# Attention with one pool of seven PSUM banks, and four and two row maxima in alternate steps

## The chip, the cores and the metric

The kernel runs on one core of a Trainium2 chip. The metric is the device time of one execution in microseconds; three executions of the kernel before took 3544.29 to 3546.45 us, with a median of 3546.07. The engines are TensorE (PE; its weight loads are shown as PEld), VectorE (DVE), ScalarE (ACT), GpSimd (POOL) and SyncE (SP, which here only issues DMAs). TensorE writes to PSUM, which has eight banks of 512 floats on each of 128 partitions; VectorE and ScalarE read it.

## The reference

Two layers of two sublayers each, on 2048 rows of 512 values in float32:

```python
x = x + fnet(layernorm(x))       # Re(DFT over rows of the DFT over columns)
x = x + attention(layernorm(x))  # 32 query heads of 16, one key head, one value head
# and both once more

q = heads(x @ wq); k = x @ wk; v = x @ wv
p = softmax(q @ k.T / 4)          # for each head, 2048 x 2048
o = concat(p @ v) @ wo
```

The softmax takes the row maximum off before the exponential, so each score is computed twice: once with queries on the partitions, for the maximum of each row, and once with keys on the partitions, for the exponential and the product with v.

## The kernel before, in words

Instructions are issued in the order in which the Python code names them; each engine works through its own in that order, and waits are put in where data or a buffer is not ready. There are two functions for each layer. `phase_a` computes the Fourier sublayer, the layer norms, and q, k and v. `phase_b` is the attention. Where a matmul of `phase_a` leaves room, `pump` and `issue` (lines 445 to 493) already put in some of the row maxima, by an estimate of when banks come free.

`phase_b` (line 1132) walks through 16 query tiles of 128 rows, and through each tile in 32 steps: two halves of the heads, times 16 tiles of 128 keys. One step has, in this order:
- the value product of two steps earlier (`pv`, line 987): four matmuls in four column groups of the array, into the one bank `z`, where they add up over the 16 key tiles;
- four score matmuls (`score`, line 963), each on 64 of the 128 array rows, so that two can run side by side on the two row halves. Two of them fill the two banks of one `pair()`, and one exponential on ScalarE (line 983) reads both;
- row maxima for later query tiles (`more_max`, line 950): one score matmul on one row half into a bank `y`, and one `reduce_max` on VectorE (line 409).

The maxima are kept at a steady rate: `owed` gives three for each step and six ahead. In a step the order is two scores, two maxima, two scores, one maximum. The row half of the first score is chosen such that matmuls go to the two halves by turns.

PSUM is divided by name: three banks `y` in rotation, two pairs `x` of two banks each in rotation, and one bank `z`. A matmul into a bank waits until the last reader of that bank's former content is done; the wait sits on the weight load ahead of the matmul.

Once for each query tile, in step 13, `o_proj` multiplies the former tile's result with the output weights: twelve matmuls into a bank `y`, and an addition on VectorE (line 1056). Where all maxima are done (the end of the last tile), the second pair of scores goes to two banks `y`, with one exponential for each (lines 971 to 976).

At the end of `phase_a`, four row tiles (12 to 15) are handled more finely: `root`, `ln_inv` and `apply` give their layer norm, `tr` transposes them through bank `z`, `q_half` computes queries, and `q_split` splits them into a rounded part and a low part that GpSimd computes (line 376). `keep` takes a bank `y` ahead of time for k, v or q, and `kept` hands it out.

Of the kernel before, what the change touches and what calls it, by code (L numbers as in the profile page):

```python
# [17 lines left out]
P = 128  # L18
# [29 lines left out]
def fnet_mqa_kernel(ctx: ExitStack, tc: tile.TileContext, x_in, ct, dt_, wq, wkv, wo, out):  # L48
# [6 lines left out]
    def f(ap):  # L55
        return ap.bitcast(F32)
# [139 lines left out]
    def make_layer(L, src, mid, dst, last):  # L196
# [76 lines left out]
                split_ps(v[0], xth, xtl)  # L273

        def keep(after):
            st["pk"], st["kept"] = bank("y"), 3
            held("y", clk["pe"] + 1.4 + 2.8 + after)

        def kept():
# [47 lines left out]
        def q_mm(tb, g, xth, xtl):  # L327
            wh, wl = st["wqh", g]
            pq = kept()
            spend(pe=2.9, act=1.2)  # L330
            for k in range(NK):
                ks = slice(k * P, (k + 1) * P)
                mm3(pq, wh[:, ks], wl[:, ks], xth[:, k, :], xtl[:, k, :], k == 0, k == NK - 1)
            hi = half(4 + 2 * (g % 2), F32R)
            lo = half(5 + 2 * (g % 2), F32R)
            split_act(pq, hi, lo, sb.tile([P, D], F32, name="qraw"))
            st["qs", tb, g] = hi, lo

        def q_half(t0, g, xth, xtl, between=lambda: None):
# [26 lines left out]
        def q_split(t0, g, pq):  # L366
            if g == 0:
                st["raw"] = half(6)
                if t0 == 14:
                    st["stage"] = slot(3, F32R)  # L370
            hl = half((4, 5, 0, 1)[g], F32R) if t0 == 12 else st["stage"][:, g * 512:(g + 1) * 512]
            raw = st["raw"][:, 256 * (g % 2):256 * (g % 2) + 256]
            nc.scalar.copy(raw, pq)
            nc.scalar.copy(hl[:, :256], raw)
            st["qs", t0, g] = hl
            sub = lambda: nc.gpsimd.tensor_sub(hl[:, 256:], raw, f(hl[:, :256]))
            (st["subs"].append(sub) if t0 == 14 and g > 1 else sub())

        def q_half_store(t0, g):
            hl = st["qs", t0, g]  # L380
# [22 lines left out]
            return o.mxp[i]  # L403

        def max_of(i, pr, g, c0, n, to, tag="y"):
            pm = bank(tag)[:, :n]
            gs = slice(64 * g, 64 * g + KR)
            nc.tensor.matmul(pm, o.qT[i][gs, pr, :], kz[gs, c0:c0 + n], start=True, stop=True)  # L408
            nc.vector.reduce_max(to, pm, axis=AX.X)  # L409
# [268 lines left out]
        def prep_tasks(tb, x1):  # L678
# [42 lines left out]
            ts[6, 0] = [lambda: (kv_lo(4 * tb, 4), k_diff(tb) if tb < 2 else None), hold]  # L721
# [11 lines left out]
        def phase_a(extra):  # L733
            tasks = {}

            def add(n, fn):
                tasks.setdefault(n, []).append(fn)
# [116 lines left out]
            for n in range(128):  # L854
# [47 lines left out]
                if n % 32 == 31 and tb < 3:  # L902
# [33 lines left out]
            take(mb, 99)  # L936
            max_neg(0, 0, HALF, 5)
            max_rows_pe(0, 0, HALF)
            for sub in st["subs"]:
                sub()  # L940
            for k in range(6):
                more_max()

# [8 lines left out]
                max_half(*units[o.done])  # L952
                o.done += 1

        def owed(n):
            return min(3 * (n + 1) + 6, len(units)) - o.done

        def done_with(i, pr):
            return all(u[:2] > (i, pr) for u in units[o.done:])
# [3 lines left out]
        def score(i, s_, j):  # L963
            hf, c = divmod(s_, NT)
            jj, g = divmod(j, 2)
            cp = 4 * (2 * hf + jj)
            if (i, s_) not in ptiles:
                k = i * NSTEP + s_
                ptiles[i, s_] = slot((6, 7, 2)[k % 3]).rearrange("p (j n) -> p j n", j=4)
            w = j // 2  # L970
            if i == NT - 1 and jj == 1 and o.done == len(units):
                e = bank("y")
                nc.tensor.matmul(e, kz[64 * g:64 * g + KR, c * P:(c + 1) * P],
                                 o.qT[i][64 * g:64 * g + KR, cp:cp + 4, :], start=True, stop=True)
                nc.scalar.activation(ptiles[i, s_][:, j, :], e, AF.Exp, scale=DH ** -0.5)
                return
            first = "e" not in st
            if first:
                st["e"] = pair()
            nc.tensor.matmul(st["e"][:, g, :], kz[64 * g:64 * g + KR, c * P:(c + 1) * P],  # L980
                             o.qT[i][64 * g:64 * g + KR, cp:cp + 4, :], start=True, stop=True)
            if not first:
                nc.scalar.activation(ptiles[i, s_][:, 2 * w:2 * w + 2, :], st.pop("e"), AF.Exp, scale=DH ** -0.5)  # L983

        acc = {}

        def pv(i, s_):
            hf, c = divmod(s_, NT)
            if c == 0:
                acc[i, hf] = bank("z")  # L990
            a = acc[i, hf]
            pt = ptiles.pop((i, s_))
            for j in range(4):
                nc.tensor.matmul(a[32 * j:32 * j + 32, :], v1[:, c, :], pt[:, j, :], start=c == 0, stop=c == NT - 1)  # L994
# [48 lines left out]

        def o_mm(k):
            if k == 0:
                bt["po"] = bank("y")
# [85 lines left out]
        def phase_b(nxt):  # L1132
# [5 lines left out]
                nc.sync.dma_start(st["wo", j], wo[:, j, :])  # L1138

            behind = []  # L1140
            for n in range(NT * NSTEP):
                i, s_ = divmod(n, NSTEP)
                if len(behind) == 2:
# [43 lines left out]
                nxt.a_start()  # L1187
            for at in behind:
                pv(*at)
            return {**out_tasks(NT - 1), 12: [lambda: o_proj(NT - 1)]}  # L1190

        def half_tasks(i):
# [63 lines left out]
```

## Time and profile before

| what | value |
|---|---|
| median of three executions | 3546.07 us |
| profiled execution, its own time | 3549.72 us |
| its span | 3547.9 us |
| TensorE busy | 3505.9 us, 99% |
| VectorE busy | 2714.7 us, 77% |
| ScalarE busy | 2503.3 us, 71% |
| first and last value product of all | 640.7 and 3538.1 us |

Times in the profile's rows are microseconds from the start of the span; the number after a bar and a comma is the mean duration of one instruction in nanoseconds. "idle before <- X" is the time in which the engine stood still just before these instructions, and X is what ended it. A matmul's end is modelled, so that a busy TensorE may still have room; the distance between the starts of equal instructions is the surer measure.

### The profile page before, as it was taken

How to read it: one execution, taken by the hardware profiler on the slowest of the kernel's cores; microseconds unless marked ns; L12 is line 12 of the kernel's file. 1: busy time of each engine (PE TensorE's matmuls, PEld its weight loads, DVE VectorE, ACT ScalarE, POOL GpSimd, SP SyncE). 2: the span in 40 equal slices, each digit the busy share in tenths (PEclk: the TensorE clock that was granted, in tenths of full speed). 3: DMA queues.
4: the chain of work that ended last, by engine and by line, in shares of the span. 5: the costliest groups of instructions: out<-in, count | busy, mean ns of one | idle time of the engine just before them, and what ended most of it. 6: DMA issues, size and time to landing. Idle time of an engine off the chain costs nothing.

```text
span 3547.9 us, 64282 instructions
## 1 busy us (share of the span) xinstructions
PE 3505.9 (99%) x24576; PEld 1874.8 (53%) x24576; DVE 2714.7 (77%) x4892; ACT 2503.3 (71%) x3210; POOL 830.5 (23%) x1262
## 2 busy tenths in 40 slices
PE   8999999999999999999999999999999999999999
PEld 6887878433333333333378878883333333333333
DVE  6267776888888888888432777768888888888883
ACT  4223733888888888888932247438888888888888
POOL 4244342211221122112213443422101110111011
PEclk9999999999999999999999999999999999999999
DMA  6435252311111100111144342523111111011100
GB/s 191 150 144 167 80 165 87 85 56 34 35 35 51 36 23 23 49 34 26 40 137 128 127 150 90 153 66 88 47 37 35 49 34 38 23 35 37 37 23 25
DMA packets 224900, 254.55 MB, mean 72 GB/s; under 512 B 52880, under 2 KB 174800, under 8 KB 217424
## 3 DMA queue, kind: packets, MB, share of 16 engines
q1 hardware_dynamic: 210384, 233.12, 21.6%
q0 software_dynamic: 14208, 17.33, 1.6%
q8 instruction: 193, 3.16, 0.4%
q14 instruction: 115, 0.94, 0.1%
HBM read 187.16 MB, written 65.27 MB: 71 GB/s over the span
## 4 chain that ended last, share of the span: by engine, by line
PE 91%; issue 2%; DVE 2%; ACT 2%; POOL 1%; DMA 1%; SPq 0%; ACTq 0%; POOLq 0%; DVEq 0%
PE z L994 29%; PE x L980 19%; PE y L408 13%; PE x L809 11%; PE y L87 3%; PE y L88 3%; PE y L89 2%; PE y L475 2%; PE x L87 2%; PE x L89 2%; PE x L88 2%; PE x L593 1%; PE z L475 1%; DVE row L191 1%; POOL cl L79 1%
## 5 line engine op out<-in xcount | busy, mean ns | idle before, releaser
L983 ACT ACTIVATE slot<-x 128x1024 f32<-128x1024 f32 x2000 | 1945.9, 1024 | 284.5 <-PE x L980 276.2
L409 DVE TENSOR_REDUCE mxp<-y 128x1 f32<-128x512 f32 x2944 | 1849.6, 684 | 181.5 <-PE y L408 168.7
L994 PE MATMUL z<-slot,v 128*32 128x512 f32 x8192 | 1096.3, 605 | 1.6 <-DVE lnv L1105 0.7
L980 PE MATMUL x<-slot,kz 64*128 64x512 f32 x2976 | 677.3, 450 | 2.2 <-DMA slot<-craw 1.7
L980 PEld LDWEIGHTS x<-slot,kz 64*128 64x128 f32 x2976 | 279.2, 184 | 744.7 <-ACT slot L983 685.8
L408 PE MATMUL y<-kz,slot 64*128 64x512 f32 x2176 | 581.6, 397 | 1.9 <-DVE mxp L409 1.9
L809 PE MATMUL x<-cl,xnh 64*128 64x512 f32 (+1 forms) x1536 | 355.8, 357 | 0.0
L994 PEld LDWEIGHTS z<-slot,v 128*32 128x32 f32 x8192 | 163.4, 108 | 363.7 <-issue 332.8
L809 PE MATMUL x<-ch,xnh 64*128 64x512 f32 (+1 forms) x1536 | 348.1, 361 | 2.3 <-ACT row L796 2.2
L809 PE MATMUL x<-ch,xnl 64*128 64x512 f32 (+1 forms) x1536 | 346.2, 362 | 0.9 <-ACT xnl L580 0.9
L408 PEld LDWEIGHTS y<-kz,slot 64*128 64x128 f32 x2176 | 276.7, 186 | 22.8 <-DVE mxp L409 10.8
L79 POOL TENSOR_TENSOR cl<-craw,ch 128x512 fp32r<-128x512 f32 x176 | 223.9, 1295 | 225.5 <-ACT ch L78 174.3
L78 ACT CAST ch<-craw 128x512 fp32r<-128x512 f32 x256 | 154.6, 622 | 170.9 <-PE x L89 87.1
L475 PE MATMUL y<-kz,slot 64*128 64x512 f32 x690 | 271.7, 405 | 2.1 <-ACT rel L479 1.2
L543 POOL DMA_DIRECT2D slot<-mt x224 | 112.1, 508 | 585.2 <-PE y L408 490.1
L809 PEld LDWEIGHTS x<-ch,xnh 64*128 64x128 f32 x1536 | 213.1, 188 | 23.3 <-issue 5.2
L809 PEld LDWEIGHTS x<-cl,xnh 64*128 64x128 f32 x1536 | 217.7, 188 | 12.6
L489 DVE TENSOR_REDUCE mxe<-y 128x1 f32<-128x512 f32 x316 | 198.8, 679 | 29.3 <-PE y L475 28.7
L809 PEld LDWEIGHTS x<-ch,xnl 64*128 64x128 f32 x1536 | 209.7, 187 | 21.1 <-issue 5.9
L1035 POOL TENSOR_TENSOR row<-row,row 128x256 f32<-128x256 f32 x63 | 46.5, 738 | 700.3 <-DMA row<-rd 654.0
L87 PE MATMUL x<-ch,xnh 128*128 128x512 f32 x384 | 154.3, 402 | 9.1 <-ACT ch L78 8.4
L89 PE MATMUL x<-ch,xnl 128*128 128x512 f32 x384 | 153.4, 399 | 2.6 <-POOL xnl L659 2.6
(198 smaller groups left out, 4143.3 us busy)
## 6 DMA issues: line engine op xcount, KB each, us to landing
craw<-ct_in SPq DMA_DIRECT2D x112, 512.0 KB
slot<-qd SPq DMA_DIRECT2D x44, 1024.0 KB
qd<-row SPq DMA_DIRECT2D x144, 128.0 KB
od<-row SPq DMA_DIRECT2D x252, 64.0 KB
row<-wqd SPq DMA_DIRECT2D x48, 256.0 KB
row<-x_in SPq DMA_DIRECT2D x32, 256.0 KB
mid<-row POOLq DMA_DIRECT2D x32, 256.0 KB, 2.4
craw<-ct_in SPq DMA_DIRECT2D x32, 256.0 KB
```

What stands on the lines that cost most here:

```text
L79: (eng or nc.vector).tensor_sub(lo, raw, f(hi))
L87: nc.tensor.matmul(ps_, ah, bh, start=start, stop=False)
L88: nc.tensor.matmul(ps_, ah, bl, start=False, stop=False)
L89: nc.tensor.matmul(ps_, al, bh, start=False, stop=stop)
L408: nc.tensor.matmul(pm, o.qT[i][gs, pr, :], kz[gs, c0:c0 + n], start=True, stop=True)
L409: nc.vector.reduce_max(to, pm, axis=AX.X)
L475: nc.tensor.matmul(pm, o.qT[i][gs, pr, :], k[gs, c0:c0 + 512], start=True, stop=True)
L489: nc.vector.reduce_max(to, pm, axis=AX.X)
L809: nc.tensor.matmul(z[d], a[gs, s, d * P:(d + 1) * P], b[gs, :], start=first and q < 2 and e == 0, stop=last and q > 1 and e == len(turns) - 1)
L980: nc.tensor.matmul(st["e"][:, g, :], kz[64 * g:64 * g + KR, c * P:(c + 1) * P], o.qT[i][64 * g:64 * g + KR, cp:cp + 4, :], start=True, sto ...
L983: nc.scalar.activation(ptiles[i, s_][:, 2 * w:2 * w + 2, :], st.pop("e"), AF.Exp, scale=DH ** -0.5)
L994: nc.tensor.matmul(a[32 * j:32 * j + 32, :], v1[:, c, :], pt[:, j, :], start=c == 0, stop=c == NT - 1)
```

## The change

- PSUM becomes one tile of eight banks. Bank 7 is `z`. In `phase_a`, `pair()` hands out banks 0 and 1, then 2 and 3, by turns, and `bank("y")` hands out 4, 5 and 6 by turns; a bank that `keep` has taken is now passed over (`own`) until its last reader is issued.
- In `phase_b`, scores, maxima and the output projection share banks 0 to 6. Which ones is decided while the program is built, by an estimate of when TensorE's two halves, VectorE and ScalarE are free (`flow`, `take_bank`, `issue_at`). A maximum takes, of the banks that are free by then, the one that came free last; if none is free, the one that comes free first. A pair takes the two neighbours that come free first.
- A step has four, two or no maxima in place of three (`share`). Credit grows in each step by what is needed to meet the next deadline, by 2 at least; at 4 or more the step takes four, else two. The order of scores (s) and maxima (m) is `smmssmms`, `ssmmss` or `ssss`.
- In the last steps, without maxima, every pair of scores has one exponential.
- At the end of `phase_a`, the maxima keep off bank `z` from the middle of task 122 until the transposes of row tile 13 are issued; `root(15)` is issued ahead of the first `q_half(12)`; and the low parts of the first two query groups of tiles 12 and 13 are computed on VectorE, after the second `q_half`.

```diff
+ORDER = {0: "ssss", 2: "ssmmss", 4: "smmssmms"}
...
+    banks = ps.tile([P, 8, 512], F32, name="banks")
+    turns = {"y": 4, "x": 0, "own": None}
...
     def bank(tag):
-        return ps.tile([P, 512], F32, name=tag, bufs={"y": 3, "z": 1}[tag])
+        if tag == "z":
+            return banks[:, 7, :]
+        while True:
+            b = turns["y"]
+            turns["y"] = 4 + (b - 3) % 3
+            if b != turns["own"]:
+                return banks[:, b, :]
...
+    def take_bank(g):
+        fb = flow["free"]
+        t = max(flow["last"], *(flow["half"] if flow["wide"] or g is None else flow["half"][g:g + 1]))
+        ready = [b for b in range(7) if fb[b] + 0.06 <= t and g is not None]
+        return max(ready, key=lambda b: fb[b]) if ready else min(range(7), key=lambda b: fb[b])
+
+    def issue_at(g, bs):
+        h = flow["half"]
+        t = max(h[g], flow["last"], *(flow["free"][b] + 0.06 for b in bs))
+        if flow["wide"]:
+            t = max(t, *h)
+            h[:] = [max(v, t) + 0.195 for v in h]
+            t = h[g]
+            flow["wide"] = False
+        h[g], flow["last"] = t + 0.231, t
+        return t + 0.431
...
     def pair():
-        return ps.tile([P, 2, 512], F32, name="x", bufs=2)
+        turns["x"] ^= 2
+        return banks[:, turns["x"]:turns["x"] + 2, :]
...
         def max_of(i, pr, g, c0, n, to, tag="y"):
-            pm = bank(tag)[:, :n]
+            if flow:
+                b = take_bank(g)
+                ready = issue_at(g, [b])
+                at = max(flow["dve"], ready)
+                flow["dve"], flow["free"][b] = at + 0.605, at + 0.69
+                pm = banks[:, b, :n]
+            else:
+                pm = bank(tag)[:, :n]
...
-            add(123, lambda: tr(13))
+            add(123, lambda: (tr(13), st.update(hold=False)))
+            inner[122, 1] = [lambda: st.update(hold=True)]
...
             tr(14)
+            root(15, 1)
             q_half(12, 0, *xt[0])
-            root(15, 1)
             ln_inv(*st["root"], nc.vector)
             apply(15)
             q_half(12, 1, *xt[0])
+            lows(2)
...
+        def share(n):
+            need = max((c - o.done) / max(1, at - 1 - n) for c, at in goals if at > n or c > o.done)
+            st["due"] = min(st.get("due", 0.0) + max(2.0, need), 6.0)
+            k = 4 if st["due"] >= 4 else 2
+            st["due"] -= k
+            return k
...
             if first:
-                st["e"] = pair()
+                b = min(range(6), key=lambda b: max(flow["free"][b:b + 2]))
+                bs = [b, b + 1]
+                ready = issue_at(g, bs)
+                st["bs"], st["e"] = bs, banks[:, b:b + 2, :]
...
-                g = units[o.done][2] if o.done < len(units) else 1
-                for j, m in ((g, 0), (1 - g, 2), (2 + g, 0), (3 - g, 2)):
-                    score(i, s_, j)
-                    for _ in range(m):
-                        if owed(n) >= 1:
-                            more_max()
+                js = iter((1, 0, 3, 2))
+                for m in ORDER[share(n) if o.done < len(units) else 0]:
+                    more_max() if m == "m" else score(i, s_, next(js))
```

More of the change, by code (lines that the diff above doesn't have):

```diff
@@ L62, in half, with start_flow, own @@
         return sb.tile([P, D], dtype, name=f"row{k}")
+    banks = ps.tile([P, 8, 512], F32, name="banks")
+    turns = {"y": 4, "x": 0, "own": None}
     def bank(tag):
[L65 removed]
+        if tag == "z":
[5 more added lines that the diff above has]
+                return banks[:, b, :]
+    flow = {}
+    def start_flow():
+        flow.update(free=[0.0] * 7, half=[0.0, 0.0], last=0.0, dve=0.0, act=0.0, wide=False, exps=[])
+    def take_bank(g):
[13 more added lines that the diff above has]
+        return t + 0.431
+    def own(ap=None):
+        turns["own"] = None if ap is None else 4 + (turns["y"] - 5) % 3
+        return ap
     def pair():
[L68 removed]
+        turns["x"] ^= 2
+        return banks[:, turns["x"]:turns["x"] + 2, :]
     def split_ps(ps_, hi, lo, neg=False):
@@ L275, in keep @@
         def keep(after):
-            st["pk"], st["kept"] = bank("y"), 3
+            st["pk"], st["kept"] = own(bank("y")), 3
             held("y", clk["pe"] + 1.4 + 2.8 + after)
@@ L953, in more_max @@
                 o.done += 1
-        def owed(n):
-            return min(3 * (n + 1) + 6, len(units)) - o.done
+        goals = []
+        for j in range(NT):
+            for lim in (HALF, NPAIR):
+                at = NSTEP * (j - 1) + NSTEP - AHEAD if j < NT - 2 or lim == HALF else NSTEP * j + NT - AHEAD
+                if j == 0:
+                    at = NT - AHEAD
+                goals.append((sum(u[0] < j or (u[0] == j and u[1] < lim) for u in units), at))
+        def share(n):
[4 more added lines that the diff above has]
+            return k
         def done_with(i, pr):
@@ L970, in score @@
             w = j // 2
[L971 to L976, printed above, removed]
             first = "e" not in st
             if first:
-                st["e"] = pair()
+                b = min(range(6), key=lambda b: max(flow["free"][b:b + 2]))
+                bs = [b, b + 1]
+                ready = issue_at(g, bs)
+                st["bs"], st["e"] = bs, banks[:, b:b + 2, :]
+            else:
+                ready = issue_at(g, [])
+            for b in st["bs"]:
+                flow["free"][b] = 1e9
             nc.tensor.matmul(st["e"][:, g, :], kz[64 * g:64 * g + KR, c * P:(c + 1) * P],
@@ L982, in score @@
             if not first:
+                at = max(flow["act"], ready + 0.03)
+                flow["act"] = at + 0.925
+                for b in st["bs"]:
+                    flow["free"][b] = at + 1.02
+                flow["exps"].append(at + 1.02)
                 nc.scalar.activation(ptiles[i, s_][:, 2 * w:2 * w + 2, :], st.pop("e"), AF.Exp, scale=DH ** -0.5)
@@ L992, in pv @@
             pt = ptiles.pop((i, s_))
+            t = max(flow["half"]) + 0.093
+            if len(flow["exps"]) > 2:
+                t = max(t, flow["exps"][-3] + 0.06)
+            flow.update(half=[t + 0.908] * 2, last=t + 0.908, wide=True, dve=flow["dve"] + 0.05)
             for j in range(4):
@@ L1045, in o_mm @@
             if k == 0:
-                bt["po"] = bank("y")
+                if flow:
+                    b = bt["pb"] = take_bank(None)
+                    bt["po"] = banks[:, b, :]
+                    t = max(*flow["half"], flow["free"][b]) + 0.19 + 12 * 0.231
+                    flow.update(half=[t] * 2, last=t, wide=True, dve=max(flow["dve"], t) + 0.69)
+                    flow["free"][b] = flow["dve"] + 0.1
+                else:
+                    bt["po"] = bank("y")
             ks = slice(k * P, (k + 1) * P)
```

15 lines of the change are left out of this document (10 added, 5 removed).

## The prediction

> **What bounds the kernel now.** I read the page first: busy time, the chain, the costliest groups.
>
> ```profile
> span 3547.9 us, 64282 instructions
> PE 3505.9 (99%) x24576; PEld 1874.8 (53%) x24576; DVE 2714.7 (77%) x4892; ACT 2503.3 (71%) x3210; POOL 830.5 (23%) x1262
> ...
> PE 91%; issue 2%; DVE 2%; ACT 2%; POOL 1%; DMA 1%; SPq 0%; ACTq 0%; POOLq 0%; DVEq 0%
> ...
> L983 ACT ACTIVATE slot<-x 128x1024 f32<-128x1024 f32 x2000 | 1945.9, 1024 | 284.5 <-PE x L980 276.2
> L409 DVE TENSOR_REDUCE mxp<-y 128x1 f32<-128x512 f32 x2944 | 1849.6, 684 | 181.5 <-PE y L408 168.7
> L994 PE MATMUL z<-slot,v 128*32 128x512 f32 x8192 | 1096.3, 605 | 1.6 <-DVE lnv L1105 0.7
> ```
>
> 91% of the chain that ended last is TensorE. ScalarE and VectorE have gaps, and those end on score (L980) and maximum (L408) matmuls. So TensorE leads and the other two follow. 2944 reductions are 1472 maxima a layer. Next the split by stretches, for the middle of layer 0's attention and for its end, where no maxima are left:
>
> ```profile
> core 0: us, PE busy (x) PEld busy (x) DVE busy (x) ACT busy (x) POOL busy (x), PEclk, DMA share, GB/s
> 500.00:700.00 200.00, 193.07 (x1793) 138.37 (x1795) 146.79 (x290) 110.37 (x186) 53.78 (x66) 0.97 0.31 90
> 1200.00:1400.00 200.00, 200.00 (x1377) 75.64 (x1374) 176.04 (x308) 173.86 (x186) 40.30 (x87) 1.00 0.11 30
> 3500.00:3537.00 37.00, 36.29 (x232) 12.67 (x232) 1.37 (x3) 35.92 (x58) 1.86 (x3) 1.00 0.11 30
> ```
>
> In the middle TensorE has no gap while VectorE is at 88% and ScalarE at 87%. Then one step in order of time (start, duration, engine, line, count):
>
> ```profile
> 1200.82 1.07 PE L994 MATMUL z<-slot,v 128*32 128x512 f32 x8
> ...
> 1201.82 0.50 PE L980 MATMUL x<-slot,kz 64*128 64x512 f32 x2
> 1201.92 0.19 PEld L408 LDWEIGHTS y<-kz,slot 64*128 64x128 f32 x2
> 1202.15 0.40 PE L408 MATMUL y<-kz,slot 64*128 64x512 f32 x2
> ...
> 1202.39 0.40 PE L980 MATMUL x<-slot,kz 64*128 64x512 f32 x2
> 1202.40 0.18 PEld L408 LDWEIGHTS y<-kz,slot 64*128 64x128 f32 x1
> 1202.41 1.94 ACT L983 ACTIVATE slot<-x 128x1024 f32<-128x1024 f32 x2 [0.18 <-PE x L980]
> 1202.58 1.89 DVE L409 TENSOR_REDUCE mxp<-y 128x1 f32<-128x512 f32 x3 [0.23 <-PE y L408]
> 1202.62 0.38 PE L408 MATMUL y<-kz,slot 64*128 64x512 f32 x1
> ...
> 1202.94 1.06 PE L994 MATMUL z<-slot,v 128*32 128x512 f32 x8
> ...
> 1205.07 1.07 PE L994 MATMUL z<-slot,v 128*32 128x512 f32 x8
> ```
>
> A step runs from one value product (L994) to the next: 2.12 and 2.13 us, mean 2.125. Inside it are four slots, in each of which both row halves of the array can work. Slot A begins 1.00 after the value product, B 0.33 later, C 0.24, D 0.23, and the next value product 0.32 after D. Slot D holds one maximum, so half of it is empty. That half is what the change is after.
>
> **The new steps without waits.** Two maxima with four scores fill three slots exactly: 1.00 + 0.33 + 0.24 + 0.32 = 1.89 us. Four maxima fill four slots: 2.12. The mean would be 2.005, and 0.12 less in about 970 steps would be worth some 115 us. VectorE's three reductions in 1.89, of 0.684 each, come 0.60 apart, and ScalarE's two exponentials in 1.94, of 1.024 each, come 0.92 apart, so six of the one (3.6) and four of the other (3.7) fit in two steps of 4.01. Neither engine's load forbids the gain. PSUM does.
>
> **The wait in the step of four.** Its order is score, max | max, score | score, max | max, score (slots A to D). At D, these banks are taken:
> - the first score pair, two banks: complete only with slot B, and its exponential lasts 1.02;
> - the second pair, two banks, opened in slot C;
> - the maxima of A, B and C, three banks.
>
> That is all seven, so the fourth maximum has to wait for the first one to be read, whichever bank the estimate names. The maximum of A is out 0.50 after the slot's start (as the scores of A at 1201.82), VectorE starts 0.03 after a matmul's end (1202.15 + 0.40 to 1202.58), and its reduction lasts 0.68: free at 1.00 + 0.50 + 0.03 + 0.68 = 2.21. Slot D would have begun at 1.80. What follows such a late release is shown by one of the few disturbed steps of before:
>
> ```profile
> 676.45 1.28 DVE L409 TENSOR_REDUCE mxp<-y 128x1 f32<-128x512 f32 x2
> ...
> 677.78 0.18 PEld L408 LDWEIGHTS y<-kz,slot 64*128 64x128 f32 x1 [0.26 <-DVE mxp L409]
> 677.78 0.49 PE L408 MATMUL y<-kz,slot 64*128 64x512 f32 x1
> ...
> 678.20 0.16 PEld L994 LDWEIGHTS z<-slot,v 128*32 128x32 f32 x8 [0.24 <-issue]
> ```
>
> The reduction ends at 677.73, the weight load goes 0.05 later, its matmul lasts 0.49 in place of 0.39 since the load is no longer hidden, and the next value product starts 0.42 after the load. So the step of four lasts 2.21 + 0.05 + 0.42 = 2.68 us. Queued behind the waiting load on TensorE are the last score and the next value product. ScalarE then waits for that score.
>
> Bounds for this wait: from below none (2.12, if a bank came free in time); from above the bank of the second maximum, read 0.60 later (3.28). I take 2.68, because at D no bank is free earlier than the first maximum's.
>
> The first row says that the exposed load costs 0.10. The Trainium skill ("TensorE: Matmul & The Clock Gate", the section on what happens when a matmul is issued) says that the queue pulls weight loads ahead of running matmuls. By that rule the step would be 2.58 and the sum below some 50 us less. Here the wait sits on the load itself, and the row at 677.78 contradicts the rule for this case.
>
> Other waits are absorbed. The second pair needs two adjacent banks in slot C and may have to wait for the preceding step's last exponential. That only shifts C, and D waits longer anyway. In the step of two, its two maxima and two pairs meet banks read long before; I take nothing, with bounds 0 and 0.10 a step (an exposed load).
>
> **How many steps.** The six maxima ahead of the attention leave 1466. Carrying the credit rule of `share` through its list of deadlines gives 246 steps of four, 241 of two and 25 of none (246 x 4 + 241 x 2 = 1466). Before, it is 488 of three, one of two and 23 of none.
>
> Per layer: 246 x (2.68 - 2.125) = +136.5; 241 x (1.89 - 2.125) = -56.6. One working step less is some -0.5.
>
> **The end without maxima.**
>
> ```profile
> 3502.76 1.04 ACT L983 ACTIVATE slot<-x 128x1024 f32<-128x1024 f32 x1
> 3502.87 0.21 PEld L994 LDWEIGHTS z<-slot,v 128*32 128x32 f32 x8 [0.24 <-issue]
> ...
> 3503.66 1.12 ACT L975 ACTIVATE slot<-y 128x512 f32<-128x512 f32 x2
> ...
> 3504.77 0.20 PEld L994 LDWEIGHTS z<-slot,v 128*32 128x32 f32 x8 [0.24 <-issue]
> ```
>
> Each step takes 1.90 there, set by one wide and two narrow exponentials. Two wide ones at 0.92 are 1.84: 25 x -0.06 = -1.5 a layer.
>
> **The output projection.** It now takes the bank that comes free first. Its row addition (0.69) stands ahead of the reductions on VectorE:
>
> ```profile
> L1056 DVE TENSOR_TENSOR row<-y,row 128x512 f32<-128x512 f32 x12 | 8.3, 691 | 38.4 <-issue 28.7 <-PE y L89 9.7
> ```
>
> Where a step of four follows, its first reduction is late by about 0.2 + 0.69 - 0.53 = 0.36 (0.2 is my estimate of when the addition starts, 0.53 is from above); in some 8 of 15 tiles: +3 a layer.
>
> **The edits of the first phase.**
>
> ```profile
> 586.96 0.66 PE L268 MATMUL z<-ident,row 128*128 128x128 f32 x4 [1.70 <-DVE mxp L489]
> ...
> 617.51 0.73 POOL L376 TENSOR_TENSOR row<-row,row 128x256 fp32r<-128x256 f32 x1 [1.16 <-ACT row L374]
> ...
> 618.47 0.16 DVE L158 TENSOR_TENSOR lnw<-lnw,lnv 128x1 f32<-128x1 f32 x1 [0.21 <-POOL lnv L150]
> ...
> 620.08 0.63 PE L268 MATMUL z<-ident,row 128*128 128x128 f32 x4 [0.68 <-DVE row L191]
> ```
>
> Keeping maxima off bank z ahead of the transposes of row 13 removes the 1.70 (the displaced maxima go to the other banks, beside matmuls). Issuing the last root sooner, with two low parts moved off GpSimd's queue, takes up to 0.68. Together -2.3 a layer; bounds -2.4 and, if the two low parts (0.73 on GpSimd, shorter on VectorE) came onto the path, +1.5. The kept bank that others skip: nothing, since the rotation before already held back.
>
> **Sum.** Per layer +136.5 - 56.6 - 0.5 - 1.5 + 3 - 2.3 = +78.6; two layers +157. The profiled execution took 3549.7 us (span 3547.9), so 3707; the median of 3546.1 is 3.6 lower, so about 3703.
>
> **Rivals.** (1) *The gain comes*: a bank is free when slot D begins. Then the step of four is 2.12 (246 x -0.005 = -1.2 a layer) and the total 3546 - 2 x (1.2 + 56.6 + 0.5 + 1.5 + 2.3) = about 3422. It decides where the stall in the step of four stays under 0.23, the gain in the step of two. For it: 88% and 87% leave room. Against: the count of seven, and 0.50 + 0.03 + 0.68 from start to release against 0.80 between A and D. 7%. (2) *The load stays hidden*: 2.58 in place of 2.68, so 3703 - 2 x 246 x 0.10 = about 3654. Against it stands the row at 677.78. 18%. (3) *The order of the step of two costs*: its halves come as 1, 0, 0, 1, 1, 0, not strictly by turns, and if a load behind its own half's matmul is exposed, 0.10 in 482 steps, about 3751. Against: the loads at 1201.92 run while both halves work. 8%. (4) *The clock falls*: with short idle gaps as in the stretch at 0.97, 3% of TensorE's own work (at most 4.01 us in two steps, 487 such pairs) is about +59: 3762. Against: 1.00 at 3500 to 3537, where TensorE waits in every step. 4%. The Trainium skill ("TensorE: Matmul & The Clock Gate", the section on a second failure mode, cycling through PSUM) says that short idle spells from such cycling make the clock gate oscillate; by that rule the loss would be larger than this rival's.
>
> **Numbers.** The forecast itself has 62%; its own range is 3675 to 3735. With (2), (3) and most of (4) the range is 3645 to 3760. A change under 0.2% (7 us) could not be told from none here. Faster 0.07, from (1); same 0.01, for a stall that happens to equal the gain; slower 0.92, from the forecast and the other three.
>
> **What would show it.** Value products alternately 2.68 and 1.89 apart; a weight load of L408 with 0.3 to 0.5 us of idle ended by a reduction, once per step of four; VectorE and ScalarE at about 80% in the middle stretch. Wrong if the steps of four are near 2.1, or if those of two show waits of their own.

## The result, and the profile after

Four executions of the kernel before on this chip have a median of 3546.26 us (3544.29 to 3546.98). Four of the changed kernel have 3757.68 us (3755.86 to 3759.89). The ratio is 1.0593, with an interval of 1.058 to 1.0605: slower by 211 us. The forecast was 3703, 157 us slower. The time lies inside the range of 3645 to 3760, but outside the forecast's own range of 3675 to 3735. That it lies inside the wide range is partly luck, as the part on the prediction shows. So the direction and the mechanism have to be looked at separately from the size.

The first view is the page of the changed kernel: span, busy time, the chain that ended last, and three of the costliest groups (in the changed kernel L457 is the matmul of a maximum, L458 its reduction, L1043 a score, L1051 the exponential, L1066 the value product).

```profile
span 3754.1 us, 64409 instructions
...
PE 3618.1 (96%) x24576; PEld 1890.6 (50%) x24576; DVE 2719.4 (72%) x4896; ACT 2551.7 (68%) x3162; POOL 825.1 (22%) x1258
...
PE 77%; DVE 12%; issue 5%; ACT 3%; POOL 1%; DMA 1%; SPq 0%; ACTq 0%; DVEq 0%; POOLq 0%
...
L1051 ACT ACTIVATE slot<-banks 128x1024 f32<-128x1024 f32 x2048 | 2030.5, 1026 | 445.7 <-PE banks L1043 369.0
L458 DVE TENSOR_REDUCE mxp<-banks 128x1 f32<-128x512 f32 x2944 | 1850.7, 684 | 351.2 <-PE banks L457 297.5
...
L457 PEld LDWEIGHTS banks<-kz,slot 64*128 64x128 f32 x2176 | 331.5, 184 | 215.0 <-DVE mxp L458 180.7
```

TensorE's share of the chain fell from 91% to 77%, and VectorE's rose from 2% to 12%. The other two engines wait longer than before, and still for TensorE's matmuls. The last row is new in its size: weight loads of the maxima stood still for 215.0 us, and most of that (180.7) ended with a reduction. The same group in the page of the kernel before:

```profile
L408 PEld LDWEIGHTS y<-kz,slot 64*128 64x128 f32 x2176 | 276.7, 186 | 22.8 <-DVE mxp L409 10.8
```

The stretch by windows that had no gap on TensorE before, with the same columns (stretch, length, busy time of PE, PEld, DVE, ACT and POOL, granted clock, DMA share, GB/s), in the changed kernel:

```profile
1200.00:1400.00 200.00, 192.98 (x1256) 70.53 (x1257) 162.36 (x285) 162.58 (x167) 36.31 (x78) 1.00 0.10 27
```

TensorE now has gaps, VectorE and ScalarE went from 88% and 87% to 81%, and the granted clock is 1.00 as before. A step of four in order of time (start, duration, engine, line, operation, count, idle time before and what ended it):

```profile
1112.45 1.06 PE L1066 MATMUL banks<-slot,v 128*32 128x512 f32 x8
...
1113.44 0.50 PE L1043 MATMUL banks<-slot,kz 64*128 64x512 f32 x1
1113.45 0.40 PEld L457 LDWEIGHTS banks<-kz,xnl 64*128 64x128 f32 x2
...
1114.02 1.89 DVE L458 TENSOR_REDUCE mxp<-banks 128x1 f32<-128x512 f32 x3 [0.40 <-PE banks L457]
1114.14 0.18 PEld L1043 LDWEIGHTS banks<-slot,kz 64*128 64x128 f32 x1 [0.29 <-ACT slot L1051]
...
1114.76 0.18 PEld L457 LDWEIGHTS banks<-kz,xnl 64*128 64x128 f32 x1 [0.43 <-DVE mxp L458]
...
1114.77 0.49 PE L1043 MATMUL banks<-slot,kz 64*128 64x512 f32 x1
1115.19 0.16 PEld L1066 LDWEIGHTS banks<-slot,v 128*32 128x32 f32 x8 [0.24 <-issue]
```

This is the predicted step. Slot A begins 1.00 after the value product. VectorE takes up the first maximum at 1114.02. The fourth maximum's weight load goes at 1114.76, after 0.43 of idle time that a reduction ended. The next value product starts 0.43 later: the step lasts 2.74 us. A second stall, which the prediction said would be absorbed, is in it too: the second score pair (1114.14) waits for an exponential.

All steps of a kernel, grouped by the number of maxima in them (the distance between starts of value products, worked out from the trace; median, and the count of steps under 3 us):

```
                    three maxima     two             four            none
before              2.126  x944      -               -               1.900  x44
after               -                1.891  x468     2.743  x440     1.833  x48
forecast            2.125 (before)   1.89            2.68            1.84
```

### The profile page after: what moved, and what is told of

Same layout as the page of the kernel before. It is cut to its first block, busy times and chain, and to the rows that moved or that the text cites. A ratio compares the mean times of both kernels' runs of the same rounds, so it can differ in the third digit from the quotient of the medians.

```text
span 3754.1 us, 64409 instructions
## 1 busy us (share of the span) xinstructions
PE 3618.1 (96%) x24576; PEld 1890.6 (50%) x24576; DVE 2719.4 (72%) x4896; ACT 2551.7 (68%) x3162; POOL 825.1 (22%) x1258
## 4 chain that ended last, share of the span: by engine, by line
PE 77%; DVE 12%; issue 5%; ACT 3%; POOL 1%; DMA 1%; SPq 0%; ACTq 0%; DVEq 0%; POOLq 0%
PE banks L1066 26%; PE banks L1043 14%; PE banks L858 10%; PE banks L457 10%; DVE mxp L458 9%; PE banks L124 4%; PE banks L126 4%; PE banks L125 4%; PE banks L524 3%; ACT slot L1051 1%; DVE row L228 1%; POOL cl L116 1%; DVE row L1070 1%; DVE row L1135 0%; PE banks L642 0%
## 5 line engine op out<-in xcount | busy, mean ns | idle before, releaser
L1051 ACT ACTIVATE slot<-banks 128x1024 f32<-128x1024 f32 x2048 | 2030.5, 1026 | 445.7 <-PE banks L1043 369.0
L458 DVE TENSOR_REDUCE mxp<-banks 128x1 f32<-128x512 f32 x2944 | 1850.7, 684 | 351.2 <-PE banks L457 297.5
L1066 PE MATMUL banks<-slot,v 128*32 128x512 f32 x8192 | 1102.0, 605 | 2.2 <-DVE lnv L1184 0.8
L1043 PE MATMUL banks<-slot,kz 64*128 64x512 f32 x3072 | 962.7, 456 | 8.4 <-DVE mxp L458 4.5
L457 PE MATMUL banks<-kz,slot 64*128 64x512 f32 x2176 | 748.9, 444 | 64.8 <-DVE mxp L458 33.6
L1043 PEld LDWEIGHTS banks<-slot,kz 64*128 64x128 f32 x3072 | 415.7, 184 | 739.7 <-ACT slot L1051 624.4
L457 PEld LDWEIGHTS banks<-kz,slot 64*128 64x128 f32 x2176 | 331.5, 184 | 215.0 <-DVE mxp L458 180.7
L858 PE MATMUL banks<-cl,xnh 64*128 64x512 f32 (+1 forms) x1536 | 361.7, 355 | 0.0
L858 PE MATMUL banks<-ch,xnl 64*128 64x512 f32 (+1 forms) x1536 | 352.2, 360 | 0.2 <-ACT xnl L629 0.2
L858 PE MATMUL banks<-ch,xnh 64*128 64x512 f32 (+1 forms) x1536 | 350.2, 359 | 2.2 <-ACT row L845 2.2
L524 PE MATMUL banks<-kz,slot 64*128 64x512 f32 x864 | 339.6, 406 | 9.9 <-DVE kraw L352 4.6
L1066 PEld LDWEIGHTS banks<-slot,v 128*32 128x32 f32 x8192 | 167.0, 108 | 316.2 <-issue 295.6
L524 PEld LDWEIGHTS banks<-kz,slot 64*128 64x128 f32 x864 | 159.6, 185 | 34.1 <-issue 9.5
L1043 PE MATMUL banks<-xnl,kz 64*128 64x512 f32 x512 | 164.6, 456 | 0.1
```

What stands on the lines that cost most here:

```text
L524: nc.tensor.matmul(pm, o.qT[i][gs, pr, :], k[gs, c0:c0 + 512], start=True, stop=True)
L858: nc.tensor.matmul(z[d], a[gs, s, d * P:(d + 1) * P], b[gs, :], start=first and q < 2 and e == 0, stop=last and q > 1 and e == len(turns) - 1)
```

## The experiments

My theory was the count of banks: eight matmuls of a step (four scores and four maxima) need eight banks beside `z`, there are seven, so the fourth maximum waits until the first is read. Its rivals: the new choice of banks does the harm, not their number; the exponentials, which hold two pairs of banks, set the step; and the order of the work within the step does. A last question was the 54 us between forecast and result. Where no interval is given, the time is that of a single execution, beside 3545.87 to 3548.39 for the kernel before on the same chip as each run. Steps are compared by their median length between two value products. No run gave the step an eighth bank; the count was tried by taking a matmul away. Where a run's kernel has lines more than the changed kernel, the line numbers in its rows are higher by one to three.

**Three maxima a step again, all else of the change kept.**

```diff
-                js = iter((1, 0, 3, 2))
-                for m in ORDER[share(n) if o.done < len(units) else 0]:
+                g = units[o.done][2] if o.done < len(units) else 1
+                js = iter((g, 1 - g, 2 + g, 3 - g))
+                left = min(3 * (n + 1) + 6, len(units)) - o.done
+                for m in "ss" + "m" * min(2, left) + "ss" + "m" * min(2, max(0, left - 2)):
```

> The changed kernel with three maxima a step again, at the rate and in the order of the kernel before; the pool of seven banks, the estimate, the wide exponentials at the end and the edits of the first phase stay. Theory A (the fourth maximum of a step has no bank): seven matmuls fill seven banks, so steps are 2.12 to 2.13 us again; with 1 us from the wide exponentials and 0.8 to 1.8 us of each first phase the time is 3540 us, 3534 to 3546. Theory B (the pool or its estimate costs something itself, by badly chosen banks): steps above 2.16 and over 3570 us.

Measured: 3542.67 us, ratio to the kernel before 0.9993 (0.9984 to 1.0002). Its steps of three last 2.127. So the pool, the estimate and the first phase's edits cost nothing that can be measured, and win nothing either. The whole loss comes with the rhythm of four and two.

**Four and two, with the banks in a fixed rotation (maxima and output projection in 4, 5, 6; pairs from 0 and 2).**

```diff
-                b = take_bank(g)
+                b = turns["y"]
+                turns["y"] = 4 + (b - 3) % 3
...
-                b = min(range(6), key=lambda b: max(flow["free"][b:b + 2]))
+                turns["x"] ^= 2
+                b = turns["x"]
...
-                    b = bt["pb"] = take_bank(None)
+                    b = bt["pb"] = turns["y"]
+                    turns["y"] = 4 + (b - 3) % 3
```

> The changed kernel with four and two maxima, but with banks in fixed rotation: maxima and output projection by turns in banks 4, 5 and 6, pairs by turns in 0-1 and 2-3, as before. Theory A: the fourth maximum waits for the first one's reduction here too, since it follows it in the rotation; steps of 2.74 and 1.89, total 3740 to 3775 us. Theory B (the estimate picks badly): well below 3700 us.

Measured: 3747.08 us; steps of four 2.738, of two 1.889. Which bank the estimate names makes no difference to the step of four: at slot D no name is a free bank.

**Reductions over half the columns.** The maxima are then too small, and the exponential's scale is lowered so that its results stay finite.

```diff
-            nc.vector.reduce_max(to, pm, axis=AX.X)
+            nc.vector.reduce_max(to, pm[:, :256] if flow else pm, axis=AX.X)
...
-..., AF.Exp, scale=DH ** -0.5)
+..., AF.Exp, scale=DH ** -0.5 / 64)
```

> The changed kernel with each reduction of the attention over the first 256 of its 512 columns (half the keys are left out of those maxima, and the exponential's scale is divided by 64 so that nothing overflows). Matmuls, banks and order stay. Theory A (the step of four ends with the release by the first reduction): the reduction falls from 0.69 to about 0.43, the steps of four from 2.74 to 2.48, those of two stay at 1.89; total 3757 - 492 x 0.26 = 3630 us or some 10 lower, since reductions queue less behind the copy of the value sum. Theory C (the step of four is long for a cause on TensorE or by the exponentials): 3745 to 3760 us.

Measured: 3671.64 us. A step of two and one of four from its trace:

```profile
1299.62 1.06 PE L1066 MATMUL banks<-slot,v 128*32 128x512 f32 x8
...
1301.00 0.19 PEld L457 LDWEIGHTS banks<-kz,slot 64*128 64x128 f32 x2 [0.20 <-ACT slot L1051]
...
1301.66 1.06 PE L1066 MATMUL banks<-slot,v 128*32 128x512 f32 x8
...
1303.23 1.43 DVE L458 TENSOR_REDUCE mxp<-banks 128x1 f32<-128x256 f32 x4 [0.62 <-PE banks L457]
...
1303.71 0.18 PEld L457 LDWEIGHTS banks<-kz,slot 64*128 64x128 f32 x1 [0.31 <-DVE mxp L458]
...
1304.13 0.16 PEld L1066 LDWEIGHTS banks<-slot,v 128*32 128x32 f32 x8 [0.24 <-issue]
```

The step of four is 2.47 long, 0.27 less than with whole reductions, and one reduction is 0.27 shorter (0.42 for 0.69). The step follows the first reduction one for one, as the theory has it. The total missed what was expected by some 40 us, because the steps of two grew from 1.89 to 2.035: their maxima (1301.00) now wait for an exponential. The estimate still reckons with reductions of 0.69; that this is why it names a bank which an exponential still reads is argued, not shown.

**No fourth maximum** (its place in the step stays empty, the tile of the maxima is set to zero on GpSimd once for each query tile, the scale is lowered as above).

```diff
+                ms = 0
                 for m in ORDER[share(n) if o.done < len(units) else 0]:
-                    more_max() if m == "m" else score(i, s_, next(js))
+                    ms += m == "m"
+                    if m == "m" and ms == 4:
+                        o.done += o.done < len(units)
+                    elif m == "m":
+                        more_max()
+                    else:
+                        score(i, s_, next(js))
```

> The changed kernel without the fourth maximum of each step of four: neither its matmul nor its reduction is issued (the maxima are set to zero first, and the exponential's scale is divided by 64). The half slot stays empty. Theory A: no eighth bank is wanted, the steps of four are 2.12 and those of two 1.89; total 3757 - 492 x 0.62 - 20 = 3430 us, 3420 to 3450. Theory C (TensorE's four slots, the alternation or the exponentials make the step long): above 3650 us.

Measured: 3597.25 us, a clear miss. The steps that lost the fourth maximum came down to 2.122, as expected, but the steps of two rose to 2.16. Two steps together take 4.28, more than 4.25 before, although they hold one maximum less. The wait had only moved. So the count of banks explains the step of four, but it is not all that stands between this plan and 4.01. What holds the steps of two was tried with the exponentials and with the choice of banks. In this run and the others without the fourth maximum, layer 0's attention is 10 to 14 us longer than layer 1's (0.4 in the kernel before). Reductions wait there for the zeroing (in the run with half exponentials and banks in rotation, below, 7 times in layer 0, 18.7 us in all, against 7.0 us in layer 1), so the lengths of steps tell more than the whole times.

**No fourth maximum, and exponentials over half of the columns** (the value product reads the computed half twice).

```diff
-..., ptiles[i, s_][:, 2 * w:2 * w + 2, :], st.pop("e"), AF.Exp
+..., ptiles[i, s_][:, 2 * w:2 * w + 2, :256], st.pop("e")[:, :, :256], AF.Exp
...
-..., v1[:, c, :], pt[:, j, :], start=
+..., v1[:, c, :], pt[:, j, :256].unsqueeze(1).to_broadcast([P, 2, 256]), start=
```

> As the first run without the fourth maximum, with each exponential over the first 256 columns of its two banks (half the exponentials are left out, and the value product reads the other half twice; matmuls, banks and order stay as in that run). Theory A4 (behind the wait for the fourth maximum's bank stands a second one: the banks of the step's second pair, whose exponential ends too late for the second pair of the step of two): an exponential lasts 0.6 in place of 1.02 and they follow 0.5 apart, so the step of two falls from 2.16 to 1.89 and that of three maxima stays at 2.12: 3597 - 482 x 0.27 = 3467 us, 3445 to 3485. Rival (the maxima's own banks or TensorE set the 2.16): above 3560 us.

Measured: 3505.95 us, 39 more than expected. The steps of two no longer wait for exponentials. What is left is a wait of their maxima for a reduction, which stood in about half of the steps of two with whole exponentials as well:

```profile
1299.13 1.06 PE L1067 MATMUL banks<-slot,v 128*32 128x512 f32 x8
...
1300.51 0.19 PEld L458 LDWEIGHTS banks<-kz,slot 64*128 64x128 f32 x2 [0.20 <-DVE mxp L459]
...
1301.18 1.06 PE L1067 MATMUL banks<-slot,v 128*32 128x512 f32 x8
```

In the step of two (2.05 here) the maxima wait for a reduction that has only just ended. The estimate takes, of the banks it believes free, the one that came free last, and leaves no margin where it is early. If that is the cause, the same order with banks in rotation must go without this wait.

**The same two kernels with the banks in rotation** (the edits are those of the rotation above).

> As the first run without the fourth maximum (full exponentials, scale divided by 64), with banks in fixed rotation: maxima in 4, 5, 6, pairs in 0-1 and 2-3. Theory A4 (the second pair of the step of two waits for the exponential of the second pair before it): that exponential ends at 3.80 from the first value product of a pair of steps, the slot is at 3.69, and with 0.05 to the load and an exposed load of 0.10 the step of two is about 2.15, that of three maxima 2.12; total 3580 to 3605 us, as with the estimate. Rival (the estimate's choice of banks makes the 2.16): steps of two at 1.89, below 3480 us.

> The same with exponentials over half the columns (half of them left out, the value product reads the other half twice). With the estimate the steps of two still lasted 2.04 there, since a maximum waited for a reduction. Theory A5 (that third wait comes from the estimate, which takes of the free banks the one that came free last and so leaves no margin): in fixed rotation every bank is read long before, the steps are 1.89 and 2.12, total 3506 - 482 x 0.15 = 3434 us, 3415 to 3450. Rival (seven banks do not carry five maxima in two such steps): 3490 us and more.

Measured: 3580.5 us with whole exponentials, 3440.39 with half ones. With the two before they make a square (step of three, step of two, their sum, whole time; us):

```
no fourth maximum      whole exponentials             half exponentials
banks by estimate      2.122 + 2.160 = 4.28, 3597     2.119 + 2.039 = 4.16, 3506
banks in rotation      2.229 + 2.059 = 4.29, 3580     2.116 + 1.887 = 4.00, 3440
```

The lower left: the total came out as expected, the split did not, since the step of three is the longer one there. Between 900 and 1700 us, 106 steps of two and 86 steps of three (about two thirds of the one and over half of the other) are lengthened by a second pair that waits for an exponential, though no estimate chooses the bank. In these rows two steps of two wait (1300.01 and 1304.29; 2.15 and 2.16 long), and the step of three between them lasts 2.12:

```profile
1298.29 1.06 PE L1069 MATMUL banks<-slot,v 128*32 128x512 f32 x8
...
1300.01 0.18 PEld L1046 LDWEIGHTS banks<-xnl,kz 64*128 64x128 f32 x2 [0.43 <-ACT slot L1054]
...
1300.44 1.07 PE L1069 MATMUL banks<-slot,v 128*32 128x512 f32 x8
...
1302.56 1.06 PE L1069 MATMUL banks<-slot,v 128*32 128x512 f32 x8
...
1304.29 0.19 PEld L1046 LDWEIGHTS banks<-xnl,kz 64*128 64x128 f32 x2 [0.44 <-ACT slot L1054]
```

The lower right, without a wait:

```profile
1301.03 1.06 PE L1069 MATMUL banks<-slot,v 128*32 128x512 f32 x8
...
1302.62 1.08 ACT L1054 ACTIVATE slot<-banks 128x512 f32<-128x512 f32 x2 [0.76 <-PE banks L1046]
...
1302.91 1.07 PE L1069 MATMUL banks<-slot,v 128*32 128x512 f32 x8
...
1305.03 0.64 PE L1069 MATMUL banks<-slot,v 128*32 128x512 f32 x4
```

1.88 and 2.12: the two steps of 4.01 that the prediction named as the plan without waits. In these runs they are there only when three things go at once: the fourth maximum, half of each exponential, and the estimate. Half an exponential both frees its banks sooner and leaves ScalarE less work; the runs do not separate these two.

**All four maxima, with the half exponentials.** If the exponentials also set the step of four, it must get shorter.

> The changed kernel, all four maxima, with exponentials over half of the columns as above (half the exponentials left out). Theory A: the step of four hangs on the first reduction, not on an exponential, so it stays at 2.74 although the wait for an exponential in slot C goes; only the 25 steps without maxima of each layer fall, from 1.83 to some 1.66, and the copy of the value sum waits less: 3735 us, 3715 to 3752. Rival (the exponentials' hold on four banks is what lengthens the step of four): below 3690 us.

Measured: 3730.2 us; the step of four stays at 2.741, and that of two at 1.889. In the middle of the attention (900 to 1700) the changed kernel had 137 steps of four whose second pair waited for an exponential; here there is none. That stall is indeed absorbed. The loads of the maxima wait just as often for a reduction (165 times) and longer in all, 128.3 us for 82.4. Waits of weight loads in that stretch (total us, times, longest us), in the changed kernel:

```profile
PEld banks L1043 <- ACT slot L1051: 286.4, 430, 0.9
PEld banks L457 <- DVE mxp L458: 82.4, 165, 1.1
```

With half exponentials (the waits for an exponential that are left are of the first pair, behind the value product):

```profile
PEld banks L1043 <- ACT slot L1051: 263.3, 314, 0.8
PEld banks L457 <- DVE mxp L458: 128.3, 165, 1.1
```

What the kernel gained over the changed one lies mostly elsewhere: 48 x 0.17 = 8 us in the steps without maxima (1.658 for 1.833), and some 16 in the steps with a copy of the value sum, which are treated below (34 x 0.40 and 26 x 0.10), where ScalarE's copy no longer comes behind a whole exponential.

**Another order in the step of four.**

```diff
-ORDER = {0: "ssss", 2: "ssmmss", 4: "smmssmms"}
+ORDER = {0: "ssss", 2: "ssmmss", 4: "ssmmssmm"}
```

> The changed kernel with steps of four in the order score, score | max, max | score, score | max, max. Theory A: the eighth matmul still finds no bank until the first maximum is read, and that maximum now starts one slot later (B): 1.33 + 0.40 + 0.03 + 0.69 + 0.05 + 0.43 = 2.93 us a step of four, total 3757 + 492 x 0.19 = 3850 us, 3830 to 3870. Rival (the split of a score pair over two slots is what costs): below 3757 us.

> As the run without the fourth maximum, but in the order score, score | max, max | score, score | max (the same work left out: every fourth maximum of a step of four; scale divided by 64). There the steps of four fell to 2.12 but those of two rose to 2.16. Theory A3 (the two exponentials of the step of four end too late for the second pair of the step of two, since its first pair is complete only in slot B): with the pair complete in slot A both end a quarter of a microsecond sooner, so 2.12 and 1.89, total about 3435 us, 3425 to 3465. Rival (a step of two cannot be 1.89 next to one of 2.12, for ScalarE's or VectorE's sake): about 3590 us again.

Measured: 4043.22 us with all maxima, some 190 more than expected, and 3580.56 without the fourth. With all of them the step of four takes 2.937, as expected for a wait on the same first reduction, which now comes later. So the order moves the wait and doesn't remove it. But the steps of two, whose order was not edited, lost more than those of four: about four in ten of them take 2.94 as well, and their mean went from 1.91 to 2.33, which is 456 x 0.42 = 190 us, beside 440 x 0.19 = 85 in the steps of four. One of them:

```profile
1314.96 1.06 PE L1066 MATMUL banks<-slot,v 128*32 128x512 f32 x8
...
1316.29 0.40 PE L457 MATMUL banks<-kz,slot 64*128 64x512 f32 x2
...
1316.72 1.29 DVE L458 TENSOR_REDUCE mxp<-banks 128x1 f32<-128x512 f32 x2 [0.29 <-PE banks L457]
...
1317.47 0.19 PEld L1043 LDWEIGHTS banks<-slot,kz 64*128 64x128 f32 x2 [1.22 <-DVE mxp L458]
...
1317.90 1.07 PE L1066 MATMUL banks<-slot,v 128*32 128x512 f32 x8
```

The second pair waits for the first maximum of its own step (the reduction that began at 1316.72). A likely reason is that a pair needs two neighbours and the free banks are not side by side; this is argued from the kernel and not shown, and it was not separated from the estimate's part. Without the fourth maximum two steps take 2.226 + 2.027 = 4.25, just what two steps took before: a miss of some 145 us, with waits for exponentials in both.

**The copy of the value sum wholly on ScalarE.** The steps of 3 us and more are left out of the medians above. Nearly all are steps in which the sum in `z` is copied out. One of the changed kernel:

```profile
1186.08 1.06 PE L1066 MATMUL banks<-slot,v 128*32 128x512 f32 x8
...
1187.64 0.38 ACT L1069 COPY row<-banks 128x256 f32<-128x256 f32 x1
...
1188.05 0.42 DVE L1070 COPY row<-banks 128x256 f32<-128x256 f32 x1 [0.81 <-ACT row L1069]
1188.39 1.88 DVE L458 TENSOR_REDUCE mxp<-banks 128x1 f32<-128x512 f32 x3
...
1189.13 0.18 PEld L457 LDWEIGHTS banks<-kz,xnl 64*128 64x128 f32 x1 [1.14 <-DVE mxp L458]
...
1189.56 0.16 PEld L1066 LDWEIGHTS banks<-slot,v 128*32 128x32 f32 x8 [0.25 <-issue]
```

VectorE's half of the copy stands ahead of the first reduction in its queue, and waits for ScalarE's half, which itself came behind an exponential. The first reduction starts 2.31 after the value product, not 1.57, and the step lasts 3.48.

```diff
-                nc.scalar.copy(oa[:, :256], a[:, :256])
-                nc.vector.tensor_copy(oa[:, 256:], a[:, 256:])
+                nc.scalar.copy(oa, a)
```

> The changed kernel with the value sum's copy out of PSUM wholly on ScalarE, where half of it was on VectorE, behind ScalarE's half. In the changed kernel the step with this copy lasts 3.32 us in place of 2.74 (steps of four, 36 times) or 2.12 in place of 1.89 (steps of two, 26 times). Theory A2 (VectorE's copy stands ahead of the first reduction, on which the step's end hangs): these steps fall to about 2.75 and 1.9 to 2.0, total 3757 - 36 x 0.57 - 26 x 0.2 = 3732 us, 3725 to 3742. Rival (the next value product waits for the bank of the value sum itself): no change, 3752 to 3762.

Measured: 3733.93 us, 24 less than the changed kernel. The changed kernel's trace has 34 such steps of four, of 3.46 on average, and not the 36 of 3.32 reckoned with above. They come down to 2.76, and 34 x 0.70 is those 24 us.

**The same copy with three maxima a step.**

> Three maxima a step in the pool of seven banks, with the value sum's copy wholly on ScalarE. The two steps around that copy last 2.17 and 2.22 there against 2.125. If the serial copies on two engines cause it, one copy is shorter than both and some 0.1 us of each of 62 pairs goes: 3542.7 - 6 = 3537 us, 0.2 to 0.3% under the kernel before. If ScalarE, at 87%, has no room: 3543 us or a few more.

Measured: 3545.72 us, ratio to the kernel before 0.9996 (0.9987 to 1.0005): no difference. Without the stall of the step of four the copy's place hardly matters; the step of the copy gets shorter (2.14 for 2.21), and the next one longer (2.32 for 2.22). No kernel here that computes the whole reference beats the one before by more than can be measured.

## Why the prediction was right, and what was mis-sized

**The wait in the step of four: right.** The stall is where it was put, once for each step, 0.43 us of idle time ended by a reduction. It follows the length of the reduction (2.74 to 2.47), disappears with the fourth maximum (2.12), and takes no notice of the choice of banks or of the exponentials.

**Its size: 2.743 in place of 2.68.** Term by term, from the rows at 1112.45 to 1115.19: 1.00 to slot A (as forecast), 0.57 to the reduction's start (0.53), 0.69 for the reduction (0.68), 0.05 to the load (0.05), 0.43 to the next value product (0.42). Why VectorE starts 0.07 and not 0.03 after the matmul was not isolated. 246 steps of 0.063 are 15.5 us a layer.

**The steps of two and of none: right.** 1.891 against 1.89; without maxima, 0.067 less than before against 0.06.

**"Other waits are absorbed": right for the exponential, incomplete for VectorE.** The forecast queued the output projection's addition ahead of the reductions, but not the copy of the value sum, which is on the same queue. The copy's steps cost, above their plain length, 34 x 0.72 + 26 x 0.23, and the steps behind them nothing: some 30 us in both layers, less 10 that these steps and the ones behind them cost before, so 10 a layer. This is the missed term. The run with the copy on ScalarE shows it.

**The output projection: right in size, wrong in place.** Above a plain step it costs 3.12 us where a step of four takes it, against 3.14 before, and not the 0.36 more that was forecast. Where a step of two takes it (6 tiles a layer), it costs 3.46, and where a step without maxima does (1 tile), 0.16 more than before. So it is 6 x 0.32 + 0.16 - 8 x 0.02 = 1.9 a layer in place of 3.

**The first phase: overestimated.** The way to the first value product got shorter by 0.8 us in layer 0 and by 1.9 in layer 1, not by 2.3. With three maxima a step, where these edits stand nearly alone, the whole kernel differs from the one before by less than the measurement tells.

**The sum.** Forecast for the attention of one layer: 136.5 - 56.6 - 0.5 - 1.5 + 3 = 80.9. With 15.5 for the step of four, 10 for the copies and -1.1 for the projection, it is 105.3. The trace has 104.9 and 104.1 (from the start of the first to that of the last value product, 1240.3 and 1239.1 after, 1135.4 and 1135.0 before). Between the two profiled executions the miss is 49 us: 47 of it in the attention, 2 in the first phase. The other 5 of the 54 are the distances of these executions from their medians.

**What was luck.** 3757.68 is inside the range of 3645 to 3760 by 2 us. The range reached that far for the rivals (3) and (4), at 3751 and 3762, and neither of them happened. The step of four and the copy filled that room, which is no merit of the range; the mechanism is what the prediction had right.

**The rivals.** (1) The gain did not come. The run without the fourth maximum shows more than the forecast knew: where seven banks do suffice, it still doesn't come, since the exponentials hold the pairs and the estimate leaves no margin. (2) The load was not hidden: the matmuls behind the wait last 0.49, and 2.743 lies above both values. The Trainium skill's rule ("TensorE: Matmul & The Clock Gate", the section on what happens when a matmul is issued) that loads are pulled ahead of running matmuls therefore does not show where the wait sits on the load itself; these rows do not contradict it, since it says nothing of a load that waits for a bank. (3) The order of the step of two costs nothing: 1.89. (4) The clock stayed: 1.00 in the middle stretch, a mean of 0.996 over the span against 0.995 before. The second failure mode that the Trainium skill describes on the same page (short idle spells from cycling through PSUM) was not seen here, with a gap of about 0.4 us in every second step.

## What to carry to other kernels

Before a denser order of work is tried, count for its tightest step how many buffers are taken at once and when the first one is read out; if one is missing, the step is as long as that reader's queue allows, and here no choice of names helped. Then take the first wait away on paper and look for the second: here the exponentials' hold on the pairs and the missing margin in the choice of banks each used up the gain. And list everything that stands in the reader's queue ahead of the read that now matters: a copy that cost 0.1 us where there was slack cost 0.7 where there was none.

## What the runs showed of the hardware

- A reduction from PSUM over 512 columns takes 0.69 us and over 256 columns 0.42 (the row at 1303.23 has four in 1.43); an exponential over 2 x 512 columns takes 1.02, over half of them 0.60. Halving the width saves less than half the time.
- VectorE's half of the copy out of `z` began 0.03 us after ScalarE's half had ended (1188.02 to 1188.05), with 0.81 of idle time before it, though the two read different columns of the bank. Whether the bank or the program's waits order them was not tried.
- Two stalls in one step do not add up: 137 waits for an exponential in the middle of the attention lay in front of the wait for the reduction, and taking all of them away left the step at 2.741.
